# w2's sums ahead of the fifth x, and x loaded by GpSimd behind the third closing in mixed groups

## The chip, the cores and the metric

The kernel runs on one core of one Trainium2 chip. The metric is the device time of one execution in microseconds, the median of several runs; lower is better. The profile is one execution taken by the hardware profiler.

## What is computed

The input `x` has 8 batches of 4,224 rows of 192 floats. A causal convolution over the rows (7 taps, 8 heads of 24 columns, softmaxed tap weights) gives y. Each row of y is then normalised, goes through a 192 x 768 and a 768 x 192 matrix with a relu between, and is added to y.

```python
w = softmax(weight)                      # (8 heads, 7 taps)
x_pad = concat([zeros(B, 6, D), x], axis=1)
y = einsum('hk,bskhg->bshg', w, windows_of_7(x_pad))   # (8, 4224, 192)
xn = (y - mean(y)) / sqrt(var(y) + 1e-6) * g_ln
out = y + maximum(xn @ w_ch1, 0.0) @ w_ch2
```

## The kernel before

**Groups.** The rows are cut into 18 groups (`groups`, line 70). Groups 0 to 2 are small starters (6, some left-over, and 10 rows for each of 128 partitions); groups 3 to 17 have 16 rows for each partition, two to a batch. Groups 3 to 17 are the "mixed" ones (`MIXED`). From group 3 on, an even group begins a batch (`j0` is 0): its x comes with six rows of the batch before it, which a `memset` by GpSimd on partition 0 replaces by zeros (line 164, the pad). Odd groups need no pad.

**One mixed group.** `up_mixed` makes the hidden activations with seven products instead of eight (sums of quarters of y and of w1 stand in: `ysums`, `w1sums`), in two passes: `one` over one hidden tile of 128, then `two` over two. Each product leaves PSUM by ScalarE (`evict`). Where two products have to be added, `close` does it: ScalarE copies the second product into a spare part of SBUF, and a DMA of GpSimd with an add (`add_by_dma`, line 613) puts it on top of the first. Pass `one` has three such closings, in the order c11, c22, c21. Pass `two` has two for `c11` (from `rooms[0]`, the tile `parts_cs`) and one for `c22` (from `rooms[1]`, `parts_tb`), and closes `c21` by VectorE (line 652). ScalarE then applies the relu (`relu`, line 659) to what was closed. Then `down_fast` multiplies by w2, again with seven products, from sums of the activations made by VectorE (`half_sum`, line 802) and from `w2sums`. Its first product reads `a[:, 0, 0]`, which is c11 of both passes, in the order hidden tile 2, 0, 1.

**What runs beside it.** During group g, VectorE runs the last five taps of group g+1 (`conv`, line 418), and ScalarE, in gaps of `down_fast`, the first two taps of group g+2 (lines 382 and 400), of which the second is added by GpSimd's DMAs (`add_second_tap`, line 410). y is stored to the output by SP (`store_y`), and the result is later added on top of it in DRAM by GpSimd's DMAs (`add_to_out`, line 933). In even groups GpSimd also works out the inverse square roots of two groups (`root`), in two pieces between the closings of pass `one`.

**Where x comes from.** `xg` has two buffers. SP has the load of x for group g+2 at the start of group g's iteration in the program; SP has little else to do and issues it as soon as the buffer is free, during the down product of group g-1. The pad's memset stands behind it on GpSimd; x4 is loaded by GpSimd, and x5 behind a memset of VectorE (`gate=True`).

**Order.** The schedule is manual: each engine does its instructions in the order in which the program issues them, and waits where data or a buffer is not ready. `let_in` is a one-element memset by VectorE on a tile that GpSimd writes next; it holds GpSimd until VectorE has come to that place. `sums_of_quarters` is a GpSimd subtraction: of 128 x 1152 elements for w1, of 128 x 288 for w2.

**The start.** Groups 0 to 2 have their own code in the loop (lines 1025 to 1066). In group 1's iteration VectorE runs group 2's convolution, then its transpose and statistics and part of group 3's convolution, while GpSimd makes the sums of quarters. y4 takes the buffer of y2 (the pool `y` has two).

## Time and profile before

| | us |
|---|---|
| median of 3 runs | 959.02 (958.75 to 959.05) |
| profiled execution | 960.39 |
| its span | 958.4 |
| TensorE busy | 947.0 |
| VectorE busy | 894.6 |
| ScalarE busy | 695.9 |
| GpSimd busy | 339.4 |
| x by SP, 2,112 KB, issue to landing | 16.5 (median of 14) |
| x by GpSimd, 2,112 KB, issue to landing | 16.4 (one) |
| closing from `parts_cs`, 512 KB, issue to landing | 6.9 (median of 28) |

The span is the time from the first to the last instruction in the profile; the profiled execution's own time has about 2 us around it. In the profile PE is TensorE's matmul, PEld its weight load, DVE VectorE, ACT ScalarE, POOL GpSimd and SP the sync engine; L613 is line 613 of the kernel. "A <- B" in a group of instructions is what is written and what is read; in the waits it is who waited and for whom.

### The profile page before, as it was taken

To read this page: it belongs to the slowest core of one execution; us is meant where nothing else is said; L and a number is where in the kernel's file an instruction comes from. 1 tells how busy PE (TensorE), PEld (TensorE's weight loads), DVE (VectorE), ACT (ScalarE), POOL (GpSimd) and SP (SyncE) were. 2 spreads that over 40 slices of the span, in tenths; PEclk is the share of its full clock that TensorE was granted. 3 is DMA by queue.
4 is the path that set the end of the run, shared out by engine and by line. 5 is a ranking of instruction groups with operands and counts; after the bars stand their busy time and mean duration, and the time that the engine had idled before them with its cause. 6 is when DMAs were issued, how large, how long until landed. Compare 5 with 4: busy or idle time off the path is not lost.

```text
span 958.4 us, 39172 instructions
## 1 busy us (share of the span) xinstructions
PE 947.0 (99%) x17490; PEld 725.5 (76%) x17490; DVE 894.6 (93%) x1509; ACT 695.9 (73%) x1165; POOL 339.4 (35%) x473
## 2 busy tenths in 40 slices
PE   8999999999999999999999999999999999999997
PEld 7887896877869587786858677685867768586787
DVE  8999999999999999999999999999989999999667
ACT  7755578596877969687786958778795867866461
POOL 1166622614145231633126141443217231361410
PEclk9999999999999999999999999999999999999999
DMA  9359689689697988979797897979888797777251
GB/s 205 112 189 176 108 235 272 120 191 223 127 275 135 249 158 198 209 130 271 135 254 149 213 200 128 269 141 250 157 213 170 150 252 140 175 137 128 45 91 69
DMA packets 39150, 168.91 MB, mean 176 GB/s; under 512 B 4421, under 2 KB 7622, under 8 KB 32967
## 3 DMA queue, kind: packets, MB, share of 16 engines
q0 software_dynamic: 32464, 105.26, 59.5%
q1 hardware_dynamic: 6512, 61.14, 17.6%
q8 instruction: 137, 2.24, 0.9%
q14 instruction: 31, 0.25, 0.1%
q10 hardware_dynamic: 6, 0.00, 0.0%
HBM read 38.93 MB, written 50.33 MB: 93 GB/s over the span
## 4 chain that ended last, share of the span: by engine, by line
PE 96%; ACT 1%; DMA 1%; DVE 1%; issue 0%; SPq 0%; ACTq 0%; DVEq 0%
PE ps L534 48%; PE ps L835 44%; PE ps L782 4%; DMA xg<-in_x_dram 1%; PE ps L326 1%; ACT w L364 0%; ACT room L646 0%; DVE room L802 0%; DVE y L938 0%; ACT y L382 0%; ACT spare L245 0%; PE ps L339 0%; SPq L219 0%; ACT room L524 0%; PE ps L354 0%
## 5 line engine op out<-in xcount | busy, mean ns | idle before, releaser
L418 DVE SCALAR_TENSOR_TENSOR y<-xg,taps,y 128x384 f32<-128x384 f32 (+3 forms) x720 | 364.2, 583 | 0.2
L835 PE MATMUL ps<-room,w2sums 128*32 128x256 f32 (+2 forms) x4608 | 246.6, 370 | 1.6 <-DVE room L802 0.9
L534 PE MATMUL ps<-yt,w 32*128 32x256 f32 (+2 forms) x4104 | 235.9, 379 | 0.5 <-ACT room L524 0.4
L646 ACT COPY room<-ps 128x1024 f32<-128x1024 f32 (+1 forms) x135 | 175.0, 1296 | 78.4 <-PE ps L534 78.1
L534 PEld LDWEIGHTS ps<-yt,w 32*128 32x128 f32 x4104 | 204.8, 185 | 25.9 <-issue 9.1
L835 PEld LDWEIGHTS ps<-room,w2sums 128*32 128x32 f32 x4608 | 148.3, 110 | 94.3 <-ACT room L659 5.3
L835 PE MATMUL ps<-room,w 128*32 128x256 f32 (+2 forms) x3456 | 188.5, 370 | 0.1
L802 DVE TENSOR_TENSOR room<-room 128x1024 f32<-128x1024 f32 (+2 forms) x147 | 160.6, 1168 | 20.7 <-PE ps L835 20.7
L835 PEld LDWEIGHTS ps<-room,w 128*32 128x32 f32 x3456 | 111.4, 110 | 69.1 <-DVE room L652 5.0
L534 PE MATMUL ps<-ysums,w1sums 32*128 32x256 f32 x2160 | 125.2, 379 | 0.0
L534 PEld LDWEIGHTS ps<-ysums,w1sums 32*128 32x128 f32 x2160 | 109.4, 185 | 10.7 <-ACT room L646 3.6
L933 POOL DMA_DIRECT2D out_dram<-ot x69 | 59.1, 989 | 160.8 <-ACT ot L922 104.7
L410 POOL DMA_DIRECT2D y<-tb x59 | 52.4, 1383 | 150.1 <-ACT room L841 101.9
L841 ACT COPY cs<-ps 128x256 f32<-128x256 f32 (+2 forms) x192 | 69.9, 367 | 44.2 <-PE ps L835 44.1
L659 ACT ACTIVATE room<-room 128x1024 f32<-128x1024 f32 (+1 forms) x89 | 92.9, 1072 | 3.1 <-DMA room<-parts_cs 2.9
L922 ACT ACTIVATE ot<-ot,r 128x192 f32<-128x192 f32 x232 | 93.9, 463 | 0.0
L382 ACT ACTIVATE y<-xg,taps 128x384 f32<-128x384 f32 (+3 forms) x141 | 73.1, 613 | 1.5 <-DMA xg<-in_x_dram 1.5
L841 ACT COPY room<-ps 128x256 f32<-128x256 f32 (+2 forms) x96 | 35.5, 370 | 50.7 <-PE ps L835 48.9
L449 DVE BATCH_NORM_STATS2 st<-y 128x6 f32<-128x192 f32 x264 | 70.2, 344 | 0.0
L400 ACT ACTIVATE tb<-xg,taps 128x384 f32<-128x384 f32 (+1 forms) x120 | 66.1, 629 | 0.0
L534 PE MATMUL ps<-yt,w1sums 32*128 32x256 f32 x1080 | 65.3, 380 | 0.0
L534 PE MATMUL ps<-ysums,w 32*128 32x256 f32 x1080 | 64.6, 376 | 0.0
(114 smaller groups left out, 916.0 us busy)
## 6 DMA issues: line engine op xcount, KB each, us to landing
xg<-in_x_dram SPq DMA_DIRECT2D x14, 2112.0 KB, 16.5
room<-room POOLq DMA_DIRECT2D x45, 512.0 KB, 5.1
out_dram<-ot POOLq DMA_DIRECT2D x59, 384.0 KB, 9.7
y<-tb POOLq DMA_DIRECT2D x58, 384.0 KB, 8.6
out_dram<-y SPq DMA_DIRECT2D x13, 1536.0 KB, 9.9
room<-parts_cs POOLq DMA_DIRECT2D x28, 512.0 KB, 6.9
room<-parts_tb POOLq DMA_DIRECT2D x14, 1024.0 KB, 7.6
xg<-in_x_dram POOLq DMA_DIRECT2D x1, 2112.0 KB, 16.4
```

Of the source, the lines that this page charges most:

```text
L382: nc.scalar.mul(y[g][:, 0:n, cs], xg[g][:, 0:n, cs], taps[:, h, 0:1])
L400: nc.scalar.mul(tb[g][:, 0:n, cs], xg[g][:, 1 : 1 + n, cs], taps[:, h, 1:2])
L418: nc.vector.scalar_tensor_tensor(out=y[g][:, 0:n, cs], in0=t[:, k : k + n, cs], scalar=taps[:, h, k : k + 1], in1=y[g][:, 0:n, cs], op0=AL ...
L449: nc.vector.bn_stats(out=sums[g][:, j, :], in_=y[g][:, j, :])
L534: nc.tensor.matmul(banks[:, q, i * w : i * w + w], right[rows, c, P * i : P * i + P], left[rows, :, c, :], start=(first and c == 0 and i = ...
L646: nc.scalar.activation(dst, src, AF.Relu) if relu else nc.scalar.copy(dst, src)
L659: nc.scalar.activation(c, c, AF.Relu)
L802: nc.vector.tensor_tensor(a[:, *dst, f], a[:, *left, f], a[:, *right, f], op=op)
L835: nc.tensor.matmul(dst[C * q : C * q + C, 0:w], right[:, f, C * c : C * c + C], left[:, f, q], start=(first and f == PAIR), stop=(f == PAI ...
L841: nc.scalar.copy(to[:, c], dst[:, 0:w].rearrange("p (j t) -> p j t", t=t))
L922: nc.scalar.mul(ots[g][:, j, :], ots[g][:, j, :], rstd[g][:, j : j + 1])
L933: nc.gpsimd.dma_start(out=rows[:, d0:d1], in_=src[:, d0:d1], accum_op=ALU.add)
```

## The change

`add_second_tap` with part of the heads (group 3 only) moves eight rows for each DMA instead of four, two DMAs instead of four.

In groups 4 to 15 the load of x for group g+2 leaves SP and the start of the iteration. GpSimd issues it, behind the third closing of pass `one` and ahead of the closings of pass `two`. Where group g+2 begins a batch (g even), the pad's memset follows the two closings of `two.c11`.

In group 1's iteration, w1's third sum and its `let_in` move to group 2's iteration, behind VectorE's taps of group 3. All four sums of w2 are now made there, ahead of the load of x4, and the `let_in` of the last two goes. y2 is stored by GpSimd, behind x4, instead of by SP.

```diff
--- before.py
+++ after.py
@@ -403,7 +403,8 @@
 
     def add_second_tap(g, upto=H):
         n = groups[g][2]
-        for js in (slice(j, min(j + 4, n)) for j in range(0, n, 4)):
+        step = 4 if upto == H else 8
+        for js in (slice(j, min(j + step, n)) for j in range(0, n, step)):
             ends = [v[:, js, 0 : upto * GRP] for v in (y[g], tb[g])]
             if upto == H:
                 ends = [v.rearrange("p j d -> p (j d)") for v in ends]
@@ -693,6 +694,9 @@
         p.evict(X, p.c12, True)
 
         next(ahead)
+        if 3 < g < NG - 2:
+            load_x(g + 2, nc.gpsimd, pad=False)
+
         p = two
         rooms = parts(cpool, "cs"), parts(bpool, "tb")
         p.product(Y, a11, p.b11, True, False)
@@ -705,6 +709,8 @@
                 p.close(p.c11[:, f : f + 1], X, rooms[0][:, f : f + 1], f)
             if g == 3:
                 store_y(g, nc.gpsimd)
+            elif g < NG - 2 and not groups[g + 2][1]:
+                nc.gpsimd.memset(xg[g + 2][0:1, 0:PAD, :], 0.0)
         act_scales(0, 1)
         if last:
 
@@ -1014,8 +1020,8 @@
     b11, b12, b21, b22 = quarters_of_w2()
     for g in range(NG):
         mixed, last = g in MIXED, g + 1 == NG
-        if g + 2 < NG and g not in (1, 2, 3):
-            load_x(g + 2)
+        if g == 0:
+            load_x(2)
         if mixed:
             work = up_mixed(g, ahead(g), pending)
             pending = iter(())
@@ -1040,19 +1046,21 @@
             next(root(0, True))
         elif g == 1:
             conv(2, 2)
-            let_in(w1sums[:, 2])
             transpose(2)
-            sums_of_quarters(w1sums[:, 2], w21, w1sums[:, 0])
-            store_y(2)
             first_tap(3)
             add_second_tap(3, 6)
-            load_x(4, nc.gpsimd, pad=False)
             sums_of_quarters(w2sums[:, 2], b12, b22)
             sums_of_quarters(w2sums[:, 0], b12, b11)
+            sums_of_quarters(w2sums[:, 1], b22, w2sums[:, 0])
+            sums_of_quarters(w2sums[:, 3], b21, w2sums[:, 1])
+            load_x(4, nc.gpsimd, pad=False)
+            store_y(2, nc.gpsimd)
         elif g == 2:
             conv(3, 2, 5, heads=(0, 6))
             lower_sum(2)
             conv(3, 5, K, heads=(0, 6))
+            let_in(w1sums[:, 2])
+            sums_of_quarters(w1sums[:, 2], w21, w1sums[:, 0])
         if g < 2:
             down(g)
             park(g)
@@ -1060,10 +1068,7 @@
                 moments(2)
                 finish(0)
                 conv(3, heads=(6, H))
-                let_in(w2sums[:, 1])
                 finish(1)
-                sums_of_quarters(w2sums[:, 1], b22, w2sums[:, 0])
-                sums_of_quarters(w2sums[:, 3], b21, w2sums[:, 1])
             continue
         if g > 2 and g + 2 < NG:
             store_y(g + 1)
```

## The prediction

> **What bounds the kernel now.** I read the page first, then the chain of waits in order of time, then the waits, then the timelines of GpSimd and ScalarE over one group, then the windows that show what the DMA engines moved. The page gives TensorE 947.0 of 958.4 us at full clock, so at most 11 us can be won anywhere, and a stall of TensorE lengthens the run one for one. The chain (start, duration, what) shows the rhythm and the one early gap:

> ```profile
> 107.11 0.92 issue
> 108.03 2.29 DVE room L802 x3
> 110.37 7.54 PE ps L835 x216
> ...
> 173.46 27.96 PE ps L534 x504
> 201.41 27.44 PE ps L835 x504
> ```

> A mixed group is 27.96 us of up products and 27.44 us of down products, with nothing between. At 110 us, in group 2's down product, TensorE waited 0.91 us for VectorE's half sums (the waits: "PE ps L835 <- DVE room L802", 0.9). The waits (us in total, times, longest) show what ends last where up meets down:

> ```profile
> ACT room L659 <- DMA room<-parts_cs: 2.9, 4, 1.3
> PEld ps L835 <- ACT room L659: 5.3, 14, 0.4
> ```

> The first says that ScalarE's relus of `two.c11` already wait at times for the two closings from `rooms[0]` to land. The second says that down's first weights hang on a relu. The timelines of group 4 (up starts at 173.46) give the distances, GpSimd first, then ScalarE:

> ```profile
> 188.07 0.89 POOL L613 DMA_DIRECT2D room<-room  x1
> 189.84 1.76 POOL L613 DMA_DIRECT2D room<-parts_cs  x2 [0.88 <-ACT parts_cs L646]
> 198.46 0.85 POOL L613 DMA_DIRECT2D room<-parts_tb  x1 [6.86 <-ACT parts_tb L646]
> ...
> 198.06 2.21 ACT L659 ACTIVATE room<-room 128x1024 f32<-128x1024 f32 x2
> 201.48 1.88 ACT L646 ACTIVATE room<-ps 128x2048 f32<-128x2048 f32 x1 [1.20 <-PE ps L534]
> ```

> The third closing of the first half goes out at +14.6 (offsets from the group's start), the two `parts_cs` closings at +16.4 and +17.3. They land 6.9 and 8.4 us after their issues, at +23.3 and +25.7. The relus that read them run from +24.6 to +26.8. In odd groups (group 7) the third closing goes out at +9.8: even groups have the square root's GpSimd steps in between.

> [...] Group 3's y store (1,536 KB) goes out by GpSimd at 135.9 behind two closings; those land at 140.1 and 142.6, and the windows (PE, PEld, DVE, ACT, POOL busy, PE clock, DMA share, GB/s) show the fast plain copy only from 141 us:

> ```profile
> 139.00:140.00 1.00, 1.00 (x25) 1.00 (x21) 1.00 (x3) 1.00 (x1) 0.00 (x0) 1.00 1.03 197
> 140.00:141.00 1.00, 1.00 (x24) 1.00 (x22) 1.00 (x2) 0.75 (x3) 0.00 (x0) 1.00 1.04 201
> 141.00:142.00 1.00, 1.00 (x28) 1.00 (x24) 1.00 (x3) 1.00 (x1) 0.00 (x0) 1.00 0.99 385
> ```

> [...] the nearest in the trace, x of group 5 on SP with little beside it, took 8.0. [...] beside the two w2 sums at 74.81 (4.39 us for what costs 1.68 beside transposes at 83.47), the convolution's VectorE steps took 1.15 us instead of 0.61.

> **Part 1: x by GpSimd, groups 4 to 15 (12 loads).** SP loses 12 issues of 0.37 us; no wait of TensorE traces back to SP. GpSimd gains 12 issues, by the 1,536 KB store about 0.9 us each. In an even group that ends at +16.4, when the next closing becomes ready; in an odd one GpSimd idles 5.7 us there. The buffer is free (the conv that read it ended a group earlier). The cost is in the ring. The rate of x there is known from x4, the one x load on GpSimd now: its windows from 83 to 88.7 us read 357, 372, 389, 447, 405 and 269 GB/s and sum to its 2.16 MB, so **x holds the ring 5.6 us**. A 512 KB closing moves at about 200 GB/s, 2.6 us.

> Even groups (6). Closing 3 ends moving near +18.6 and the two `parts_cs` closings follow without a gap today, ending near +24.1. With x between, both land 5.6 us later, the second at 25.7 + 5.6 = +31.3. Its relu takes 1.06: +32.36. TensorE needs that block third in down's first product. Seven products in 27.44 are 3.92 each, with nine (c, f) steps of 0.436, so it is due at 27.96 + 0.87 = +28.83. Stall 32.36 − 28.83 = **3.5 us**. Relu c12, queued behind on ScalarE (1.88 us), ends at +34.2, when TensorE comes to the bank it frees; nothing more is lost. The six stalls are 21.2 us. GpSimd's pad memset (1.05 us, now at +1.2 with x landed) comes to wait for x, landing at about +26.2. Behind it, `parts_tb`'s closing leaves near +27.2 instead of +25.0 and lands near +36.6; its relus are at +34.5 plus the 3.5 already lost, so it adds none. GpSimd's later steps wait for ScalarE anyway.

> Odd groups (6). Closings 2 and 3 stop moving at about +15.1 (windows of group 9), and the engines then idle until the pair from about +18. x fills +15.1 to +20.7, the pair ends at +25.9, lands at +27.4, and the relu ends at +28.5: 0.3 before +28.83. I take **0**, with 0 to 1 us each as bounds, since landings scatter by about 1 us.

> First taps of the new x are at +39.6, over 12 us after it lands. What gets better, the `out_dram` adds (9.4 us to land) and `y<-tb` adds (8.5) without x beside them, is waited for by nothing on TensorE's path: 0.

> **Part 2: the start.** On GpSimd w1's third sum (2.67 us at 68.51) leaves, four `y<-room` issues (5.24 us in all) become two of twice the size, two sums of w2 come forward from 83.47, then x4, then y2's store, which leaves SP. Group 3's taps end at 69.9, so the issues start there, not at 71.1. Each of the two is not shown: at least one present issue (1.3), at most two (2.6), with the overlap in dispatch seen at 71 to 74 I take 1 us in the queue. The four sums then run from about 72, at 0.7 to 0.84 each, to about 75, mostly beside VectorE's statistics and transposes and not beside its convolution at 74.8: VectorE gains up to 2.2 us (12 steps took 8.55 us, and would take 6.4 at 0.53 spacing). If they slip past 75, up to as much is lost instead. x4 leaves later but its ring is busy with `y<-room` until about 82 to 83, so it lands near 90 as now (90.6); cover gone, ScalarE's first tap at 94.33 waits. y2's store follows in the ring [...] and lands near 93; y4 takes y2's buffer at that same 94.33, so 1.3 us is left.

> Two waits of sums on a VectorE memset go, 0.06 us each; w1's new one is the same memset later. w1's sum now runs behind group 2's root on GpSimd (ends 106.6, or some 0.6 sooner) and meets the half sums that TensorE waits for. VectorE being early, these could start at TensorE's release, 107.09: **−0.9 us** without contention. With the slowing seen at 75 us (about double) three half sums take up to 4.5 instead of 2.29 and end at 111.6: **+1.3**. I take +0.5. y4's adds queue behind this sum (108.19 to 109 or 112), and land before the conv at 125.3. The sum itself is due at 124.9.

> **The sum.** 21.2 + 0 + 0.5 = +21.7 us. The profiled execution is 960.39 (span 958.4 and 2.0 around it), and would be 982.1; it stands 1.4 above the median 959.02, so the median becomes **980.7**.

> **Rivals.**
> (a) *The odd groups stall as well.* For it: 0.3 us of slack, and group 9's relu waited 1.3 already. Against: the idle gap at +15 to +18. At 1 to 3 us each, 6 to 18 us more: about 993.
> (b) *Half the stall.* x could move near 430 GB/s (5.0 us, 0.6 less) and closing 3 be through 1 us sooner: 2 us each, 12 in all, with the start's +0.5 about 971.5.
> (c) *No stall: not slower.* In the even groups x has 28.83 − 26.8, about 2.0 us, of slack before TensorE waits. If GpSimd's transfers don't stand in line, so that x costs the closing pair under 2.0 us, only the start remains, −0.9: 958.1. For it: x is hidden today, on SP's queue. Against: the windows at 139 to 142 us, and x4.
> (d) *Faster*: as (c), and the small gaps of the chain at 680 to 774 us, 1.6 us of waits, close as well: 956.5. Nothing links the edit to them.

> **How the numbers follow.** The forecast (3.5 us in even groups, nothing much in odd) has 0.58, (a) 0.14, (b) 0.17, (c) 0.09, (d) 0.02. A measurement of this kernel can tell about 0.2%, 1.9 us. (c) is all within that but for a tail: faster 0.03, same 0.07, slower 0.90. The forecast's own bounds are x at 5.0 to 6.2 us, the odd groups at 0 to 1, the start at −0.9 to +2: 975 to 991. Half of (b) and most of (a) brought in: 966 to 995.

> **What would show it.** After the change, the waits list ScalarE L659 on the `parts_cs` transfer some 4 to 5 us in each even group, and the chain has six gaps of about 3.5 us at even groups' change from up to down, none at odd ones; closings from `parts_cs` take 12 to 14 us to land in even groups; the wait at 110 us is between 0 and 2.2 us; GpSimd's pad memset waits for x. Six gaps absent with x on GpSimd's queue would make the forecast wrong, and so would gaps in the down phase or at first taps.

## The result and the profile after

The change makes the kernel slower by more than the forecast range allowed: median 1011.14 us (1009.39 to 1015.73) against 959.3 for the kernel before, a ratio of 1.0543 (95% interval 1.0521 to 1.0565). The forecast was 980.7, range 966 to 995. The profiled execution took 1011.22 us with a span of 1008.9, 50.5 more than the span before.

From the waits of the changed kernel (who waited for whom: us in total, times, longest). Lines have moved: 659 is now 660, 613 is 614, 802 is 808, 835 is 841.

```profile
ACT room L660 <- DMA room<-parts_cs: 59.2, 25, 5.6
POOL xg L713 <- DMA xg<-in_x_dram: 56.4, 6, 10.3
PE ps L841 <- ACT room L660: 33.3, 24, 2.9
PE ps L841 <- DVE room L808: 2.1, 1, 2.1
```

The first line was 2.9 us before. It is the wait that was forecast, but it comes 25 times, twice in nearly every one of the 12 groups that load x, and not only in the six even ones. The third line is the wait of TensorE that follows from it; it did not exist before.

The timeline of group 4 (up starts at 175.6), GpSimd, then TensorE (start, duration, what, idle before and its releaser):

```profile
190.27 0.89 POOL L614 DMA_DIRECT2D room<-room  x1
190.89 0.85 POOL L157 DMA_DIRECT2D xg<-in_x_dram  x1
192.03 1.77 POOL L614 DMA_DIRECT2D room<-parts_cs  x2 [0.29 <-ACT parts_cs L647]
203.04 1.05 POOL L713 MEMSET xg<- 1x1152 f32 x1 [9.24 <-DMA xg<-in_x_dram]
...
203.54 0.64 PE L841 MATMUL ps<-room,w 128*32 128x256 f32 x8
206.76 0.64 PE L841 MATMUL ps<-room,w 128*32 128x256 f32 x8 [2.58 <-ACT room L660]
209.10 4.68 PE L841 MATMUL ps<-room,w 128*32 128x256 f32 x56 [1.70 <-ACT room L660]
```

x stands between the third closing and the pair from `parts_cs`. The pair lands 13.5 and 15.0 us after its issues (6.9 and 8.4 before). TensorE does down's first (c, f) step, waits for the first block of `two.c11`, does that step, waits for the second. The last line holds a thing that was not in the forecast: 56 matmuls take 4.68 us, where the same 56 take 3.27 us in group 9. The windows show why (the seventh number is the clock granted to TensorE):

```profile
196.00:197.00 1.00, 1.00 (x28) 0.95 (x24) 1.00 (x3) 1.00 (x2) 0.00 (x0) 1.00 0.90 389
...
207.00:208.00 1.00, 0.40 (x8) 0.00 (x0) 0.96 (x1) 0.01 (x1) 0.00 (x0) 1.00 1.20 250
208.00:209.00 1.00, 0.00 (x0) 0.00 (x0) 0.00 (x0) 1.00 (x2) 0.00 (x0) 0.84 0.86 180
209.00:210.00 1.00, 0.90 (x12) 0.45 (x16) 0.92 (x1) 1.00 (x2) 0.00 (x0) 0.50 1.06 221
210.00:211.00 1.00, 1.00 (x16) 0.54 (x12) 1.00 (x3) 1.00 (x3) 0.00 (x0) 0.50 0.84 180
```

At 196 us, with x on its way since 190.89, the DMA engines move 389 GB/s. At 208.7 us, after TensorE has done one step of 8 matmuls since 204, its clock falls to half, and stays there for 3.4 us (6.8 us in groups 10, 12 and 14). The page of the kernel before showed full clock throughout (mean 1.000). The times of the changed kernel's six runs go with their mean clocks: 0.986 at 1009.39 us, 0.982 to 0.984 from 1010.57 to 1011.22, 0.977 at 1014.75 and 0.975 at 1015.73.

An odd group, 9 (up starts at 475.4), has one short stall and keeps its clock:

```profile
503.38 1.07 PE L841 MATMUL ps<-room,w 128*32 128x256 f32 x16
505.57 3.27 PE L841 MATMUL ps<-room,w 128*32 128x256 f32 x56 [1.13 <-ACT room L660]
```

From the starts of the up products, the length of each group, in us (before: 55.4, but for 56.4 and 56.6 in groups 13 and 14):

| group | 4 | 5 | 6 | 7 | 8 | 9 | 10 | 11 | 12 | 13 | 14 | 15 |
|---|---|---|---|---|---|---|---|---|---|---|---|---|
| after | 61.4 | 58.0 | 61.4 | 57.3 | 61.7 | 57.3 | 61.9 | 57.0 | 62.5 | 56.8 | 62.6 | 57.3 |

Against the kernel before, the even groups lose 38.0 us in all, the odd ones 10.3, and group 4 starts 2.1 later. That is 50.4 of the 50.5 us. The even groups' loss can be read from the starts of TensorE's steps (one step is the 8 matmuls of one (c, f) pair, 0.44 us). In each, two stalls come to 4.4 to 5.1 us, 28.2 us in all. Behind them, each step at half clock takes 0.42 us more, 11.1 us in all; some 1.2 us of gaps that group 14 had before are gone.

### The profile page after: what moved, and what is told of

It is laid out like the page before. It is cut to its first block, busy times and chain, and to the rows that moved or that the text cites. A ratio compares the mean times of both kernels' runs of the same rounds, so it can differ in the third digit from the quotient of the medians.

```text
span 1008.9 us, 39132 instructions
## 1 busy us (share of the span) xinstructions
PE 963.0 (95%) x17490; PEld 720.0 (71%) x17490; DVE 896.4 (89%) x1508; ACT 698.2 (69%) x1165; POOL 345.8 (34%) x484
## 4 chain that ended last, share of the span: by engine, by line
PE 48%; DMA 15%; POOL 8%; ACT 7%; issue 5%; DVE 1%; POOLq 0%; ACTq 0%; DVEq 0%
PE ps L841 35%; DMA room<-parts_cs 15%; PE ps L535 13%; POOL room L614 3%; ACT room L660 2%; ACT room L647 2%; ACT ot L928 1%; POOL d L462 1%; POOL d L480 1%; POOL r L485 1%; POOL d L481 1%; PE ps L788 1%; ACT cs L847 1%; DVE room L653 1%; POOL xg L157 1%
## 5 line engine op out<-in xcount | busy, mean ns | idle before, releaser
L841 PE MATMUL ps<-room,w 128*32 128x256 f32 (+2 forms) x3456 | 204.3, 388 | 32.4 <-ACT room L660 31.4
L841 PEld LDWEIGHTS ps<-room,w2sums 128*32 128x32 f32 x4608 | 144.7, 110 | 99.5 <-ACT room L660 7.1
L808 DVE TENSOR_TENSOR room<-room 128x1024 f32<-128x1024 f32 (+2 forms) x147 | 163.1, 1182 | 38.4 <-PE ps L841 37.6
L660 ACT ACTIVATE room<-room 128x1024 f32<-128x1024 f32 (+1 forms) x89 | 93.4, 1069 | 59.2 <-DMA room<-parts_cs 59.2
L535 PEld LDWEIGHTS ps<-ysums,w1sums 32*128 32x128 f32 x2160 | 108.8, 185 | 11.1 <-ACT room L647 3.6
L817 DVE SCALAR_TENSOR_TENSOR room<-room 128x1024 f32<-128x1024 f32 (+1 forms) x45 | 53.7, 1200 | 33.0 <-ACT room L660 32.3
## 6 DMA issues: line engine op xcount, KB each, us to landing
room<-parts_cs POOLq DMA_DIRECT2D x28, 512.0 KB, 11.7
```

The lines of the kernel that those rows point to most:

```text
L535: nc.tensor.matmul(banks[:, q, i * w : i * w + w], right[rows, c, P * i : P * i + P], left[rows, :, c, :], start=(first and c == 0 and i = ...
L660: nc.scalar.activation(c, c, AF.Relu)
L808: nc.vector.tensor_tensor(a[:, *dst, f], a[:, *left, f], a[:, *right, f], op=op)
L841: nc.tensor.matmul(dst[C * q : C * q + C, 0:w], right[:, f, C * c : C * c + C], left[:, f, q], start=(first and f == PAIR), stop=(f == PAI ...
```

## The experiments

Three theories were put against each other. **Theory 1**: the closing pair is late by the ring time of x ahead of it. **Theory 2**: x in the up phase loads the shared DMA engines, and its place in the queue is not the point. **Theory 3**: GpSimd is held up, by the issue or at the memset that waits for x.

**Each part alone.** The start's part, x left on SP:

```diff
-        if 3 < g < NG - 2:
-            load_x(g + 2, nc.gpsimd, pad=False)
-            elif g < NG - 2 and not groups[g + 2][1]:
-                nc.gpsimd.memset(xg[g + 2][0:1, 0:PAD, :], 0.0)
-        if g == 0:
-            load_x(2)
+        if g + 2 < NG and g not in (1, 2, 3):
+            load_x(g + 2)
```

> The start's part alone: w2's four sums ahead of x4, w1's third sum behind group 3's taps, y2 stored by GpSimd, the tap's adds in two DMAs; x of groups 6 to 17 stays on SP. Theory 1 (place in the ring of GpSimd's queue: what costs is x ahead of the closing pair): 960 to 961.5, that is +1 to +2 of the +52, from a wait of 2.1 us instead of 0.9 at the half sums of group 2. Theory 2 (the engines are shared in the up phase, wherever x stands in the queue): the same 960 to 961.5. Rival: the start shifts something that recurs in each group: 970 or more.

And x by GpSimd alone, the start as before (the same lines put into the kernel before):

> x of groups 6 to 17 by GpSimd behind the third closing, with the pad's memset behind the c11 pair; the start as in the kernel before. Both theories: about +50, 1007 to 1011, with six even groups near 61.5 us and six odd near 57.3. If the two parts add, this and the start's part alone come to the whole +52.

Measured: the start alone 961.64 us, ratio 1.0026 (1.0012 to 1.0040); x alone 1009.85, ratio 1.0522 (1.0507 to 1.0538). The parts add within the noise. x by GpSimd is 49.7 of the loss, the start about 1.5 to 2.

**x ahead of the first closing instead of behind the third.**

```diff
+        if 3 < g < NG - 2:
+            load_x(g + 2, nc.gpsimd, pad=False)
         X, Y = take_set(), take_set()
...
         next(ahead)
-        if 3 < g < NG - 2:
-            load_x(g + 2, nc.gpsimd, pad=False)
```

> The changed kernel, but GpSimd issues x at the head of up_mixed, ahead of the first closing, and not behind the third; the memset stays behind the pair. x still moves through GpSimd's ring and still in the up phase. Theory 1: x is through at about +10 us, the pair lands as in the kernel before (7 to 8.5 us after issue), all stalls go: 960 to 962. Theory 2: x still takes engine time in the up phase, closings 1 and 2 late by 6 us but with more room; the pair unaffected in this variant too, so the same. Rival 3 (GpSimd's issues or its wait at the memset cost): the memset finds x landed here, same result; a clock that stays at 1.00 in all groups is expected of all.

Measured: 963.9 us, ratio 1.0044 (1.0032 to 1.0057), clock 0.999. The same twelve DMAs, by the same engine, through the same ring, 9 to 14 us earlier, cost 2.3 us beside the start alone instead of 50. Groups 4 to 15 take 55.4 to 55.9 us. It is a little above what was expected, and why is not shown: the closings of pass `one` stand behind x now and land after 9.6 us by the median instead of 5.2, but in the profiles groups 4 to 15 together take as long as with the start alone (667 us).

**x behind the pair.**

```diff
                 p.close(p.c11[:, f : f + 1], X, rooms[0][:, f : f + 1], f)
...
+        if 3 < g < NG - 2:
+            load_x(g + 2, nc.gpsimd, pad=False)
         act_scales(0, 1)
```

> The changed kernel, but GpSimd issues x behind the two c11 closings instead of ahead of them; the pad's memset goes behind the closing from parts_tb. x moves at nearly the same time as in the changed kernel. Theory 1 (order in the ring): the pair lands 6 to 8.5 us after issue, the stall at the change from up to down goes and TensorE's clock stays at 1.00; the parts_tb closing now stands behind x, lands near +37 of the group, and its relus make TensorE wait 1 to 3 us at down's third product: about 975 to 988. Theory 2 (engines shared): the pair stays late, 12 us or more to land, and the time stays above 1000.

Measured: 1001.28 us, ratio 1.0434 (1.0421 to 1.0448), clock 0.991. The time is where theory 2 had it, above 1000, but not in theory 2's way. From this kernel's waits:

```profile
ACT room L660 <- DMA room<-parts_tb: 31.1, 12, 3.7
ACT room L660 <- DMA room<-parts_cs: 1.5, 2, 0.8
```

The pair is in time again (6.9 us to land by the median), and the lateness has gone over to the next closing, from `parts_tb`, which lands after 12.1 us instead of 7.6: once in each of the 12 groups. Groups 4 to 15 take 56.9 to 60.8 us. The stall at down's third product is theory 1's, 1.1 to 3.4 us a group and 26 us in all. What it had left out is 0.5 us at the step behind it in every group, the clock at half in groups 4, 6, 9 and 14, and a start of group 4 that is 3.6 us later than before, where the clock fell at 113.5 us behind TensorE's wait for the half sums.

**The memset out of GpSimd's way**, moved behind the closing from `parts_tb`:

> The changed kernel with the pad's memset behind the closing from parts_tb, so that GpSimd doesn't stand 9 us at it in even groups before that closing. Theory 1 (x ahead of the pair in the ring): nothing changes, 1009 to 1012, since nobody waited for the parts_tb closing. Rival 3 (GpSimd blocked at the memset): 4 to 6 us less in each even group, 975 to 985.

Measured: 1011.82 us, ratio 1.0540 (1.0524 to 1.0556). GpSimd's 56.4 us of waiting at the memset shrink to 8.6, and nothing is gained. Theory 3 falls.

**Filler for TensorE**, in even groups only:

```diff
                 for f in (PAIR, *range(PAIR)):
+                    if first and bank == 0 and c == 0 and f < PAIR and g in range(4, 16, 2):
+                        for _ in range((5, 4)[f]):
+                            for q in range(NQ):
+                                nc.tensor.matmul(
+                                    banks[1][C * q : C * q + C, 0:w], right[:, PAIR, 0:C],
+                                    left[:, PAIR, q], start=True, stop=True, ...
```

> The changed kernel; in even groups 4 to 14 TensorE gets nine extra steps of matmuls (2.2 us before the first block of two.c11, 1.7 us before the second, with results that nobody reads), which fit into the stalls of 2.8 and 1.9 us. Theory: part of the loss in even groups is TensorE's clock at 0.5 after the stall; TensorE kept busy, the clock stays at 1.00 and each even group is about 1.5 us shorter (59.8 instead of 61.4): about 1001, mean clock above 0.995. Rival (the low clock has nothing to do with TensorE being idle): 1010 to 1013, mean clock near 0.984.

Measured: 1000.79 us, ratio 1.0432 (1.0412 to 1.0452), mean clock in the profile 0.997 instead of 0.984. Its TensorE timeline in group 4 (line 843 is the filler):

```profile
204.28 2.34 PE L843 MATMUL ps<-room,w 128*32 128x256 f32 x40
207.07 0.64 PE L849 MATMUL ps<-room,w 128*32 128x256 f32 x8 [0.45 <-ACT room L660]
207.53 1.91 PE L843 MATMUL ps<-room,w 128*32 128x256 f32 x32
209.39 3.27 PE L849 MATMUL ps<-room,w 128*32 128x256 f32 x56
```

TensorE does 72 matmuls more in each even group and the kernel is 10.4 us faster than with none. The blocks come as late as before; the 56 matmuls behind them take 3.27 us instead of 4.68. So the low clock came with TensorE's idle time: with the blocks as late but TensorE busy, it was nearly gone. It was worth about 1.5 us in each even group: of the 11.2 us between the two spans, 8.9 lie in the even groups and 2.6 in the odd ones, which have no filler. No length of a stall decides on the clock alone, and TensorE need not be idle throughout: it was busy for 16 to 35% of the 3.41 us ahead of the changed kernel's six falls (the last section).

**Fewer bytes at the critical place.** 14 of x's 22 rows at the head of `up_mixed`, 8 rows (786 KB, in thousands of bytes) behind the third closing:

> The changed kernel with x in two DMAs: 14 of the 22 rows at the head of up_mixed, 8 rows (786 KB, some 2.3 us of the ring) behind the third closing. Theory 1 (the lateness of the pair is the ring time of what stands ahead of it): the pair is 2 to 3 us late instead of 6.6, even groups 0.5 to 1 us longer than 55.4, odd groups not at all, no low clock: 964 to 969. If the number of DMAs ahead of the pair counts and not their bytes: over 990.

Measured: 971.59 us, ratio 1.0123 (1.0107 to 1.0138), clock 0.999. The second of the pair lands 10.7 to 11.9 us after issue in even groups, 1.6 to 3.5 us later than in the kernel before (8.4 to 9.1), and in time in odd ones (7.3 to 8.8). Even groups take 56.3 to 57.6, odd ones 55.4 to 55.7. The lateness follows the bytes: 786 KB give 2.6 us by the mean, x's whole 2,163 KB (2,112 on the page, which counts in 1,024 bytes) gave 6.4. The time is some 3 us over what was expected, each even group up to 1.2 us over its own.

**The same moment by SP.** GpSimd writes one element of x's buffer behind the third closing, and SP's load waits for that:

```diff
-            load_x(g + 2, nc.gpsimd, pad=False)
+            load_x(g + 2, pad=False, gate=nc.gpsimd)
```

> The changed kernel with x sent by SP at the same moment: GpSimd writes one element of x's buffer behind the third closing, and SP's load waits for that. The bytes move at the same time, but in SP's ring, not in GpSimd's. If a DMA engine divides its time evenly between two rings, x (6.3 us of work) is through before closing 3 and the pair (7.8 us) in any case, and the pair lands as late as in the changed kernel: 1000 to 1010. If GpSimd's ring gets most of the turns, the pair is up to 5 us earlier: 965 to 985. Not over 1012 by either.

Measured: 1016.72 us (1009.0 to 1020.28), ratio 1.0605 (1.0569 to 1.0640). By its page the pair is as late through SP's ring, 10.9 us by the median (11.7 through GpSimd's, 6.9 before):

```profile
room<-parts_cs POOLq DMA_DIRECT2D x28, 512.0 KB, 10.9
```

So x need not stand in the closings' ring to delay them. That corrects theory 1 towards theory 2; how the engines share their time between two rings is shown by no view. On SP's ring x also slows the third closing, which was issued ahead of it: in odd groups that lands after 9.0 to 13.7 us, against 6.9 to 7.4 in the changed kernel, and through ScalarE's copies TensorE comes to wait in the up products:

```profile
ACT room L647 <- DMA room<-room: 11.7, 9, 3.1
PE ps L535 <- ACT room L647: 12.2, 8, 2.8
```

So part of this kernel's time is lost at another place. Its runs lie far apart as their clocks do: 0.990 at 1009.0 us, 0.982 at 1013.74, 0.979 and 0.978 at 1019.7 and 1020.28. In the profiled one the clock fell in groups 6, 7, 8, 11 and 14.

**The start.** Two kernels with x on SP place w1's third sum elsewhere. In the first, group 2's square root moves behind it on GpSimd, so that the sum runs beside VectorE's transpose:

```diff
-                if f == 3:
-                    next(root(2, True))
...
             sums_of_quarters(w1sums[:, 2], w21, w1sums[:, 0])
+            next(root(2, True))
```

> The start's part alone (x on SP), with group 2's root on GpSimd moved behind w1's third sum, so that this sum runs beside VectorE's transpose of group 3 (from about 102 us) and not beside the half sums that TensorE waits for. Theory (the start's cost is w1's sum contending with three half sums): TensorE's wait there falls from 2.2 us to under 0.6, 1.5 to 2 us less than the start's part alone and 0 to 1 less than the kernel before: 958.0 to 959.8 beside a before of 959.3. If the root's small steps, which then run beside the half sums, slow them as much, the wait stays near 2 us.

In the second the sum and its `let_in` stay in group 1's iteration, and only w2's sums (in that same iteration, ahead of x4) and the rest of the start have changed:

> The start's part alone, but w1's third sum and the VectorE element ahead of it stay in group 1's iteration, beside the transpose of group 2. Then w2's sums start some 2.5 us later and run into VectorE's convolution at 75 us, all four of them. Theory: VectorE loses there what the early sums had won (2 to 4 us over 12 steps), TensorE's wait at the half sums of group 2 is between 0.9 and 3 us: 959.5 to 961.5. If the half sums were slowed by something else than w1's sum, 961 or more.

The first measured 968.95 us, ratio 1.0085 (1.0068 to 1.0103). TensorE's wait at group 2's half sums went, as expected, but the root's steps, now behind the sum, pushed y4's adds to 119.3 us (109.4 with the start alone) and the sums of y behind them; TensorE then waited 1.3, 1.9 and 2.6 us in group 3, and its clock fell to 0.5 behind the second and the third of these waits; group 3 took 65.1 us instead of 55.6. The second measured 959.59, ratio 0.9997 (0.9987 to 1.0007), no different from the kernel before. The half sums in the timelines of VectorE, first with the start's part alone, then with w1's sum in its old place:

```profile
106.84 9.14 DVE L803 TENSOR_TENSOR room<-room 128x640 f32<-128x640 f32 x9 [0.38 <-PE ps L836]
```

```profile
107.79 6.74 DVE L803 TENSOR_TENSOR room<-room 128x640 f32<-128x640 f32 x9
```

The nine instructions take 2.4 us longer beside w1's sum, which GpSimd runs from 106.8 to 109.4 with the start alone. The kernel without that sum has TensorE wait 0.6 us there, the one with it 2.2 (0.9 before).

## Why the prediction was wrong

The mechanism was right: x ahead of the closing pair makes it late (11.7 us to land by the median instead of 6.9), ScalarE's relus wait for it (59.2 us), TensorE waits for the relus (33.3 us) at down's first product, in the order and at the steps named. No part went against its forecast sign, but the sizes were wrong. The sum was +21.7, measured in the profiled spans +50.5. The terms that failed:

- **"A stall of TensorE lengthens the run one for one."** This failed. The stalls in even groups brought the clock down to half for 3.4 or 6.8 us more, about 10 us in all: the even groups' 38.0 less the 28.2 of the stalls, 8.9 by the filler kernel. The prediction had put this at nothing. The longest wait of TensorE in the middle of the kernel before is about 1 us, so its profile could not show it.
- **"x holds the ring 5.6 us."** This was x4's bytes over the rate of its windows. The second of the pair landed 14.7 to 15.4 us after issue in even groups, against 8.4 to 9.1: 6.4 later by the mean. In group 4 it came at +32.3 instead of the forecast +31.3, and the stall was 4.7 us (2.8 before the first block, 1.9 before the second) instead of 3.5: 7 us over six groups. Why the lateness is 0.8 us more than the 5.6 is not shown.
- **"Odd groups: 0."** The pair's second closing was given 0.3 us of room. In group 9 it landed at +29.1 instead of the forecast +27.4, since x began to move at +15.6 and not +15.1, and after four microseconds at 372 to 439 GB/s the windows show 168 to 270. TensorE lost 1.3 us at the first product and 0.5 at the third, where it waited for ScalarE's relu too. Six odd groups: 10.3 us. Rival (a) was this case, at 6 to 18 us, and its 993 was the nearest of all; but with the clock's share it would have been 1003.
- **"Take +0.5" for the start.** Group 4 starts 2.1 us later in the profile, and the runs give 1.5 to 2. The bound of +1.3 from the doubling of VectorE's time at 75 us was the right end: TensorE's wait went from 0.9 to 2.2. The half sums took 9.14 us beside w1's sum on GpSimd and 6.74 without it. The other half of that step was right: with the start alone w2's sums ran from 71.1 to 76 us, and VectorE's 12 steps at 75 us took 6.94 us instead of 8.55.

Four errors, all in one direction: 10 + 7 + 10.3 + 1.6 = 28.9, of 28.8 missing. The 10 is what the others leave of the even groups' loss, so that the sum closes is no check of it; the filler kernel is. The range had taken the outer bounds of single terms, but held no term for a cost that follows from the stall itself.

Rivals (b), half the stall, and (c), no stall, fell. x is not hidden on SP because SP's ring is apart: sent by SP at the new moment it cost as much (1016.72 us against 1011.14), in part at another closing, and sent by GpSimd at the head of the up phase it cost some 2 us. It was hidden because it moved well before a transfer that TensorE's path waits for. That what stands behind x in GpSimd's ring lands later was the author's assumption; the windows of before at 139 to 142 us only go with it. The kernel with x behind the pair bears it out: the pair lands in time (6.9 us by the median) and the closing behind x does not (12.1 instead of 7.6).

## What to carry to other kernels

A load without urgency must not be served just ahead of a transfer that is waited for within its own length. It is the moment and the bytes that count here, on either queue: the same load 9 to 14 us earlier cost 2 us and here 50. When slack is a few tenths of a microsecond, take a transfer's time from its landing (here x made the pair 6.4 us later), not from bytes over the mean rate (5.6), and count the slack as gone. And where stalls may leave TensorE as little busy as ahead of the falls here (11 to 47% of 3.41 us), add what the lower clock costs afterwards, here 1.5 to 2.3 us for each time; matmuls that nobody reads won 10.4 us back in six groups here, but the blocks came as late as before.

## What was unexpected of the hardware

The kernel with x behind the pair has two single stalls side by side (behind the bounds come the length of the stretch and TensorE's busy time; the seventh number is the clock):

```profile
509.42:512.83 3.41, 1.24 (x21) 0.41 (x20) 2.37 (x1) 2.41 (x4) 0.00 (x0) 1.00 1.05 313
512.83:516.24 3.41, 3.41 (x40) 1.73 (x36) 0.00 (x0) 2.83 (x10) 1.52 (x2) 0.50 1.08 325
567.44:570.86 3.42, 1.79 (x36) 0.79 (x26) 3.29 (x2) 0.16 (x1) 1.01 (x2) 1.00 0.99 183
570.86:574.27 3.41, 1.87 (x32) 0.96 (x36) 0.60 (x1) 3.29 (x7) 0.04 (x1) 1.00 1.06 400
```

In group 9 a stall of 2.1 us lies in one stretch, TensorE is busy for 36% of it, and the clock falls. In group 10 a stall of 3.0 us is shared out over two stretches, busy for 52 and 55%, and the clock stays. With x by GpSimd alone, group 10 escaped in the same way with two stalls of 3.8 us in all, and took 59.8 us, where the other even groups took 61.1 to 62.8. A single stall of 2.0 us in group 5 of the changed kernel did nothing (busy for 66%); one of 1.9 us in the kernel with the root behind w1's sum did (busy for 44%). So whether a stall of 2 to 3 us met the low clock went here with where it fell in the beat, which no kernel here controls: it is luck.

And the same number of bytes on two rings of the engines delayed the pair about as much as on one (10.9 us to land by the median, 11.7 on one, 6.9 before).
